# One decode step of windowed attention and a SwiGLU branch: Q, gate and up turned by VectorE's block transposes, and the last two rows of W_O in fifteen small loads

## The chip, the cores and the metric

The kernel runs on one core of a Trainium2 chip. The metric is the device time of one execution in microseconds (us); the kernel before takes 202.76 us, the median of three runs (201.81 to 202.96).

## The reference

Four sequences, one new token each, hidden size 512. The token is normalised; an attention branch over the last 4096 positions of a cache and a gated feed-forward branch both start from it, and the sum with x is the result.

```python
# x: [4,1,512]; caches: [4, 8 kv heads, 16384, 128]; 32 query heads; F = 1792; all bfloat16
xn = layernorm(x)
q = (xn @ wq) as 32 heads of 128                    # wq: [512, 4096]
k, v = last 4096 positions of the caches, each kv head for 4 query heads
p = softmax(q @ k.T * 128 ** -0.5)
a = (p @ v) as [4, 4096] @ wo                       # wo: [4096, 512]
f = (silu(xn @ w_gate) * (xn @ w_up)) @ w_down      # w_gate, w_up: [512, 1792]; w_down: [1792, 512]
out = x + a + f
```

## The kernel before

**Loads.** SyncE issues nearly all DMA from one queue, in a written order: W_Q (4 MB), K of steps 0 and 1, W_gate, W_up, V of step 0, then K and V in turn, W_down, V of the last step in two halves, and W_O in four loads (`load_wo`, L231) of its row groups 0 to 15, 16 to 25, 26 to 29 and 30 to 31 (`WO_CUTS`, L121). A row group c is `WO[:, c, :]`: 128 partitions of 512 values, so the last load is 128 partitions of 2 KB. K and V have two buffers each; a K load waits until the transposes of two steps before are done (`s_tr`), a V load until PV of two steps before is done (`s_pv`).

**Start.** ScalarE and VectorE normalise x, TensorE turns it, and `XnT` holds it with hidden along the partitions and 32 columns, of which 4 are the tokens. Q is computed in 32 matmuls (L370 to L375) with `XnT` stationary and 512 columns of W_Q moving; four of them write the four 32-partition groups of a PSUM tile, so that the tokens are in partitions 32j to 32j+3. ScalarE and VectorE copy the two tiles to `QB`, eight TensorE transposes turn them, and four VectorE copies sort them into `QZ` (L293 to L296).

**Loop.** 16 steps (`ND`), each with one kv head of two sequences, 64 tiles of 128 positions. TensorE transposes K tile by tile into four PSUM tiles, VectorE copies them to `KT` (`evac`, L299), TensorE forms the scores; a maximum, a shift and ScalarE's exponential follow, and PV (`pv`, L413) adds P x V and the denominators. `norm` (L316) divides. The order of every engine is written out by hand, with a semaphore for each dependence.

**End.** After the last scores TensorE computes gate and up into `ps_kt[0]` and `ps_kt[1]` (L452 to L460). Column f of W_gate is seen as (m, t) with f = 14 m + t. Each of the four partition groups gets four of the 14 values of t, `T0[j]` to `T0[j] + 3` (groups 2 and 3 overlap in two), so a matmul moves 128 runs of four neighbours, 14 apart, in 512 columns. ScalarE takes exp(-gate); VectorE adds 1, takes the reciprocal, multiplies by gate and by up (L337 to L345), all on 128 partitions x 512 columns of which 4 partitions in 32 are tokens. Meanwhile TensorE does the last step's PV; then four transposes turn `gu` (L467), four turn the attention output (L471), VectorE copies both (`OB`, `guT`), four matmuls with `rep` spread the heads (L477), VectorE copies `OP`. The 28 matmuls with W_down (L483) and the 64 with W_O (L490) add into `ps_acc`, on two groups of columns side by side. Before row groups 0, 16, 26 and 30 of W_O TensorE waits for the load that brings them (L491). VectorE copies the sum to `y`, and SyncE and ScalarE store a half each.

Of the kernel before, what the change touches and what calls it, by code (L numbers as in the profile page):

```python
# [3 lines left out]
BF16 = mybir.dt.bfloat16  # L4
FP32 = mybir.dt.float32
# [5 lines left out]
def bass_parallel_sum__sliding_block_cached__swiglu_ffn__decode_kernel(  # L11
# [67 lines left out]
    st_std = sb("st_std", [B, 1], FP32)  # L79
    st_rstd = sb("st_rstd", [B, 1], FP32)  # L80
    XnT = sb("xnT", [128, NC, 32], BF16)
    QB = sb("qB", [128, 2, 512], BF16)
    den = sb("den", [128, C], FP32)
    OT = sb("oT", [128, B, REP + HQ], BF16)
    OB = sb("oB", [32, B, Dh], BF16)
    OP = sb("oP", [128, NO, B], BF16)
    ex = WQ[:, 0:1024].bitcast(FP32)
    gu = sb("gu", [128, 4, 128], BF16)
    guT = sb("guT", [128, 4, 128], BF16)
    I4 = sb("i4", [B, B], FP32)  # L90
    I4w = sb("i4w", [B, 64], BF16)
    y = sb("y_sb", [128, 256], BF16)
# [9 lines left out]
    O_wide = ps_O[:, 0:WIDE]  # L102
    den_ps = ps_O[:, 128:256]
    xT_ps = ps_acc[:, 0:NC * B]
    q_ps = kt_ps[2]
    mt_ps = ps_acc[0:C, 0:128]
    gate_ps = ps_kt[0][:]
    up_ps = ps_kt[1][:]
    gu_ps = kt_ps[2][:, B:2 * B, :]
    tr_ps = kt_ps[2][0:32, 0:B, :]  # L110
    op_ps = ps_kt[3][:, 0:B * 32]

    def sem(name):
        return nc.alloc_semaphore(name=name)
# [4 lines left out]
    d_wd = sem("d_wd")  # L119
    d_out = sem("d_out")  # L120
    WO_CUTS = (0, 16, 26, 30, 32)  # L121
    d_wo = [sem("d_wo%d" % q) for q in range(len(WO_CUTS) - 1)]
    d_k = [sem("d_k%d" % s) for s in range(2)]
    d_v = [sem("d_v%d" % s) for s in range(2)]
    d_vz = sem("d_vz")
# [7 lines left out]
    s_xT = sem("s_xT")  # L133
    s_xnT = sem("s_xnT")
    s_q = sem("s_q")
    s_qb = sem("s_qb")
    s_qt = sem("s_qt")
    s_gu = sem("s_gu")
    s_gt = sem("s_gt")
    s_qz = sem("s_qz")  # L140
    s_tr = sem("s_tr")
# [33 lines left out]
    with nc.Block() as block:  # L175
# [40 lines left out]
        @block.sync  # L216
        def _(eng):
            def load_k(d):
                if d >= 2:
                    eng.wait_ge(s_tr, 2 * NG * (d - 1))  # L220
                eng.dma_start(KB[:, d % 2 * KVN:(d % 2 + 1) * KVN], kv_ap(A_k_cache, d)).then_inc(d_k[d % 2], 16)

            def load_v(d):
                eng.wait_ge(s_pv, d + 1)
                eng.dma_start(VB[:, d % 2 * KVN:(d % 2 + 1) * KVN], kv_ap(A_v_cache, d)).then_inc(d_v[d % 2], 16)

            def load_v_half(d, h, done):
                a = d % 2 * KVN + h * HKN
                eng.dma_start(VB[:, a:a + HKN], kv_ap(A_v_cache, d)[:, :, h * HKN:(h + 1) * HKN]).then_inc(done, 16)

            def load_wo(n):  # L231
                a, b = WO_CUTS[n], WO_CUTS[n + 1]
                eng.dma_start(WO[:, a:b, :], wo_ap[:, a:b, :]).then_inc(d_wo[n], 16)

            eng.dma_start(WQ[:], wq_ap).then_inc(d_wq, 16)
            load_k(0)
            load_k(1)
            eng.dma_start(WG[:], wg_ap).then_inc(d_wg, 16)
            eng.dma_start(WU[:], wu_ap).then_inc(d_wu, 16)
            load_v(0)  # L240
            for d in range(2, ND):
                load_k(d)
                load_v(d - 1)
            eng.dma_start(WD[:], wd_ap).then_inc(d_wd, 16)
            eng.wait_ge(s_pv, ND)
            load_v_half(ND - 1, 0, d_v[1])
            load_v_half(ND - 1, 1, d_vz)
            for n in range(len(d_wo)):
                load_wo(n)
            eng.wait_ge(s_y, 1)  # L250
            eng.dma_start(out_ap[0], y[0:B, :]).then_inc(d_out, 16)
            eng.wait_ge(d_out, 32)

        @block.scalar
        def _(eng):
            eng.dma_start(X[:], x_ap).then_inc(d_x, 16)
            eng.wait_ge(s_xc, 1)
            eng.activation(xc[:], X[:], ACT.Identity, bias=st_neg[:, 0:1], scale=float(D))
            eng.drain()
            eng.activation(xsq[:], xc[:], ACT.Square, accum_out=st_sum[:, 0:1]).then_inc(s_ss, 1)  # L260
            eng.wait_ge(s_var, 1)
            eng.activation(st_std[:], st_var[:], ACT.Sqrt).then_inc(s_std, 1)
            eng.wait_ge(s_rs, 1)
            eng.activation(xn[:], xc[:], ACT.Identity, scale=st_rstd[:, 0:1]).then_inc(s_xn, 1)  # L264
            eng.wait_ge(s_q, 1)
            eng.activation(QB[:, 0, :], ps_kt[0][:], ACT.Identity).then_inc(s_qb, 1)
            for d in range(-1, ND):
                eng.wait_ge(s_sh, d + 2)
                eng.activation(P[:, d % 2 * PS:d % 2 * PS + SN], ps_S[d % 2][:], ACT.Exp, scale=SCALE).then_inc(s_p, 1)  # L269
            eng.wait_ge(s_gate, 1)  # L270
            eng.activation(ex, gate_ps, ACT.Exp, scale=-1.0).then_inc(s_ex, 1)  # L271
            eng.wait_ge(s_y, 1)
            eng.dma_start(out_ap[1], y[64:64 + B, :]).then_inc(d_out, 16)

        @block.vector
        def _(eng):
# [6 lines left out]
            eng.wait_ge(s_xT, 1)  # L283
            eng.wait_ge(s_const, 1)
            eng.tensor_copy(XnT[:, :, 0:B], xT_ps.rearrange("p (c b) -> p c b", b=B)).then_inc(s_xnT, 1)
            eng.wait_ge(s_q, 1)
            eng.tensor_copy(QB[:, 1, :], ps_kt[1][:]).then_inc(s_qb, 1)  # L287
            eng.wait_ge(s_qt, 1)

            qv = q_ps.rearrange("p (n h) (j x) -> p j n x h", n=2, x=32)  # L290
            qz = QZ[:].rearrange("p (j n i) c -> p j n i c", n=2, i=2)
            for n in range(2):
                for i in range(2):  # L293
                    last = eng.tensor_copy(qz[:, :, n, i, 0:C].rearrange("p j (m h) -> p j m h", m=2),  # L294
                                           qv[:, :, n, 2 * i:2 * i + 2, :])
            last.then_inc(s_qz, 1)  # L296
            eng.engine_nop().then_inc(s_ev, NG)

# [27 lines left out]
            with eng.Fori(0, ND // 2) as r:  # L326
                for b in range(2):
# [5 lines left out]
            row_max(1, ND + 1)  # L333
            shift(ND + 1)
            norm(ND + 1, 0, ND // 2)
            eng.wait_ge(s_ex, 1)
            eng.tensor_scalar(ex, ex, 1.0, None, ALU.add)  # L337
            eng.drain()
            eng.reciprocal(ex, ex)  # L339
            eng.drain()  # L340
            eng.tensor_tensor(ex, gate_ps, ex, ALU.mult)  # L341
            eng.wait_ge(s_up, 1)
            eng.drain()
            eng.tensor_tensor(gu[:].rearrange("p u m -> p m u"), up_ps.rearrange("p (m u) -> p m u", u=4),  # L344
                              ex.rearrange("p (m u) -> p m u", u=4), ALU.mult).then_inc(s_gu, 1)  # L345
            norm(ND + 2, 1, ND // 2)

            eng.wait_ge(s_t4, 1)
            eng.tensor_copy(OB[:], tr_ps).then_inc(s_ob, 1)
            eng.wait_ge(s_gt, 1)  # L350
            eng.tensor_copy(guT[:], gu_ps).then_inc(s_guT, 1)
            eng.wait_ge(s_pm, 1)
            eng.tensor_copy(OP[:].rearrange("p c b -> p b c"), op_ps.rearrange("p (b c) -> p b c", b=B)).then_inc(s_op, 1)
            eng.wait_ge(s_acc, 1)
# [3 lines left out]
        def _(eng):  # L358
# [8 lines left out]
            last.then_inc(s_xT, 1)  # L367
            eng.wait_ge(s_xnT, 1)
            eng.wait_ge(d_wq, 16)
            for c in range(NC):  # L370
                for n in range(2):
                    for j in range(4):
                        a = (c * HQ + 8 * j + 4 * n) * Dh
                        last = mm(ps_kt[n][32 * j:32 * j + 32, :], XnT[:, c, :], WQ[:, a:a + 512], start=(c == 0))
            last.then_inc(s_q, 1)  # L375
            eng.wait_ge(s_qb, 2)
            for k in range(8):
                last = eng.transpose(q_ps[:, k, :], QB[:, k // 4, 128 * (k % 4):128 * (k % 4 + 1)], ident[:])  # L378
            last.then_inc(s_qt, 1)

            def mask(bank):
                return mm(ps_S[bank][:].rearrange("p (t c) -> p t c", c=C), mkr[:],
# [65 lines left out]
            pv(0, 1, ND + 1)  # L448
            shift(1, ND + 1)


            T0 = (0, 4, 8, NF - 4)  # L452
            for w, o, done, d in ((WG, ps_kt[0], s_gate, d_wg), (WU, ps_kt[1], s_up, d_wu)):
                eng.wait_ge(d, 16)
                for c in range(NC):
                    wv = w[:, c, :].rearrange("p (m t) -> p m t", t=NF)
                    for j in range(4):
                        last = mm(o[32 * j:32 * j + 32, :].rearrange("p (m u) -> p m u", u=4), XnT[:, c, :],
                                  wv[:, :, T0[j]:T0[j] + 4], start=(c == 0))
                last.then_inc(done, 1)  # L460
            for n in range(2):
                mm(ps_acc[64 * n:64 * n + 64, 0:256], I4w[:], X[:, 256 * n:256 * n + 256], start=True)
            pv(1, 0, (8 * ND + 16, ND + 1))
            eng.wait_ge(d_vz, 16)
            pv(1, 1, None)
            eng.wait_ge(s_gu, 1)
            for u in range(4):  # L467
                last = eng.transpose(gu_ps[:, u, :], gu[:, u, :], ident[:])
            last.then_inc(s_gt, 1)
            eng.wait_ge(s_nrm, ND + 2)  # L470
            for i in range(B):  # L471
                last = eng.transpose(
# [5 lines left out]
                last = mm(op_ps.rearrange("p (b c) -> p b c", b=B), rep[:, e, :], OB[:, :, 32 * e:32 * e + 32],  # L478
                          start=(e == 0))
            last.then_inc(s_pm, 1)  # L480
            eng.wait_ge(s_guT, 1)
            eng.wait_ge(d_wd, 16)
            for t in range(NF):  # L483
                j = min(t // 4, 3)
                u = t - T0[j]
                for n in range(2):
                    mm(ps_acc[64 * n:64 * n + B, 0:256], guT[:, u, 32 * j:32 * j + B],
                       WD[:, t, 256 * n:256 * n + 256])
            eng.wait_ge(s_op, 1)
            for c in range(NO):  # L490
                if c in WO_CUTS:  # L491
                    eng.wait_ge(d_wo[WO_CUTS.index(c)], 16)
                for n in range(2):
                    last = mm(ps_acc[64 * n:64 * n + B, 0:256], OP[:, c, :], WO[:, c, 256 * n:256 * n + 256])
# [29 lines left out]
```

## Time and profile before

| | before |
|---|---|
| runs, us | 202.96, 202.76, 201.81 (median 202.76) |
| profiled execution, us | 203.49, of which the span of instructions 201.8 |
| granted TensorE clock, mean | 0.958 |
| HBM read | 81.01 MB, 402 GB/s over the span |
| busy share | PE 83%, PE weight loads 71%, VectorE 59%, ScalarE 9%, GpSimd 5% |
| chain that ended last | DMA 51%, PE 40%, VectorE 6%, issue 2% |

The span is the time from the first to the last instruction that the profiler records in one execution; the profiled execution's own time has some 1.7 us more around it. Busy shares are averages over stages with different limits. The chain is followed back from the last instruction, at each step to what released it. A line such as L360 is a helper's (`mm`), so groups are told apart by their tiles.

### The profile page before, as it was taken

The page shows a single profiled execution, that of the slowest core. Times are in us where ns is not written, and L with a number is a line of the kernel's source. Part 1 is how long each engine was busy: PE and PEld are TensorE (multiplying, and loading weights), DVE is VectorE, ACT ScalarE, POOL GpSimd, SP SyncE. Part 2 cuts the span into 40 slices and gives each one's busy share as a digit, 9 for nine tenths or more (in the row PEclk, how much of TensorE's full clock was granted, in tenths as well). Part 3 has the DMA queues.
Part 4 walks back from the last instruction along what each step waited for, and adds up shares of the span by engine and source line. Part 5 has one row for each costly group of instructions (what it writes and reads, how often), then busy time and mean ns, then how long its engine had stood idle before and what let it go on. Part 6 is the DMA issues. An engine that isn't in the chain of part 4 may idle for free.

```text
span 201.8 us, 7765 instructions
## 1 busy us (share of the span) xinstructions
PE 167.1 (83%) x3470; PEld 143.2 (71%) x3470; DVE 119.3 (59%) x250; ACT 17.6 (9%) x27; POOL 10.3 (5%) x23
## 2 busy tenths in 40 slices
PE   0137998859999989889898989898989898986395
PEld 0113896758988978788788878887878787854263
DVE  1003757644777575757666767676767676738700
ACT  6303010101010101010100101010101010110000
POOL 8920000000000000000000000000000000000000
PEclk9999699988999999999999999999999999999559
DMA  7999999999999999999999999999999999999800
GB/s 248 448 393 429 436 424 426 437 422 429 406 426 439 435 422 439 432 422 435 432 432 426 439 435 422 439 432 422 435 432 432 426 439 435 413 435 421 373 12 1
DMA packets 5934, 81.10 MB, mean 402 GB/s; under 512 B 668, under 2 KB 680, under 8 KB 936
## 3 DMA queue, kind: packets, MB, share of 16 engines
q1 hardware_dynamic: 5912, 81.01, 94.4%
q8 instruction: 5, 0.08, 0.2%
q10 hardware_dynamic: 16, 0.01, 0.0%
q14 instruction: 1, 0.01, 0.0%
HBM read 81.01 MB, written 0.00 MB: 402 GB/s over the span
## 4 chain that ended last, share of the span: by engine, by line
DMA 51%; PE 40%; DVE 6%; issue 2%; ACT 0%; DVEq 0%
DMA kbuf<-in_A_k_cache_dram 44%; PE ps_kt L390 17%; PE ps_s L360 9%; DMA wq_sb<-in_A_wq_dram 6%; PE ps_o L360 6%; PE ps_acc L360 5%; PE ps_kt L360 3%; DVE wq_sb L339 2%; DVE kT L302 1%; DVE gu L344 1%; DVE rm L307 0%; DVE qB L287 0%; DVE wq_sb L341 0%; PE ps_kt L378 0%; ACT wq_sb L271 0%
## 5 line engine op out<-in xcount | busy, mean ns | idle before, releaser
L302 DVE COPY kT<-ps_kt 128x1024 bf16<-128x1024 bf16 x128 | 79.8, 683 | 27.3 <-PE ps_kt L390 27.2
L390 PE MATMUL ps_kt<-ident,kbuf 128*128 128x128 bf16 x1024 | 64.4, 222 | 10.6 <-DMA kbuf<-in_A_k_cache_dram 10.5
L390 PEld LDWEIGHTS ps_kt<-ident,kbuf 128*128 128x128 bf16 x1024 | 58.8, 99 | 15.6 <-issue 15.6
L360 PE MATMUL ps_o<-p,vbuf 128*128 128x64 bf16 x1120 | 39.4, 195 | 0.0
L360 PEld LDWEIGHTS ps_o<-p,vbuf 128*128 128x128 bf16 x1120 | 36.2, 99 | 1.2
L360 PEld LDWEIGHTS ps_s<-qz,kT 128*128 128x128 bf16 x1024 | 31.4, 98 | 7.6 <-issue 4.6
L360 PE MATMUL ps_s<-qz,kT 128*128 x1024 | 34.8, 192 | 2.0 <-issue 0.8
L269 ACT ACTIVATE p<-ps_s 128x512 bf16<-128x512 f32 x17 | 10.2, 597 | 152.0 <-PE ps_s L360 152.0
L307 DVE TENSOR_REDUCE rm<-ps_s 128x8 bf16<-128x512 f32 x17 | 11.8, 691 | 19.3 <-PE ps_s L360 19.3
L360 PE MATMUL ps_kt<-wq_sb,xnT 128*32 128x512 bf16 x32 | 3.4, 609 | 5.4 <-DMA wq_sb<-in_A_wq_dram 5.4
L360 PE MATMUL ps_o<-p,ones 128*128 128x128 bf16 (+1 forms) x69 | 6.9, 220 | 0.8 <-DVE qz L294 0.7
L360 PE MATMUL ps_s<-mkc,mkr 2*128 2x512 bf16 x17 | 6.7, 393 | 0.0
L365 PE MATMUL ps_acc<-i,xn 4*128 4x4 f32 x4 | 0.6, 255 | 7.2 <-ACT xn L264 7.2
L360 PE MATMUL ps_s<-dg,ones 8*128 8x512 bf16 x17 | 6.5, 385 | 0.0
L360 PEld LDWEIGHTS ps_kt<-wq_sb,xnT 128*32 128x32 bf16 x32 | 1.3, 140 | 6.9 <-issue 6.9
L318 DVE TENSOR_REDUCE den<-ps_o 128x8 f32<-128x128 f32 x18 | 5.1, 281 | 1.6 <-PE ps_o L360 1.6
L287 DVE CAST qB<-ps_kt 128x512 bf16<-128x512 f32 x1 | 0.7, 691 | 8.7 <-PE ps_kt L360 8.7
L365 PEld LDWEIGHTS ps_acc<-i,xn 4*128 4x128 f32 x4 | 0.6, 210 | 7.2 <-issue 7.2
L360 PEld LDWEIGHTS ps_o<-p,ones 128*128 128x128 bf16 x69 | 4.5, 98 | 1.3 <-issue 0.8
L211 POOL MEMSET vbuf<- 128x6144 f32 x1 | 5.2, 5222 | 0.0
L360 PE MATMUL ps_acc<-wo_sb,oP 128*4 128x256 bf16 x64 | 5.1, 334 | 0.0
L355 DVE CAST y_sb<-ps_acc 128x256 bf16<-128x256 f32 x1 | 0.4, 426 | 7.5 <-PE ps_acc L360 7.5
(69 smaller groups left out, 62.7 us busy)
## 6 DMA issues: line engine op xcount, KB each, us to landing
kbuf<-in_A_k_cache_dram SPq DMA_DIRECT2D x16, 2048.0 KB, 12.6
vbuf<-in_A_v_cache_dram SPq DMA_DIRECT2D x15, 2048.0 KB, 11.2
wq_sb<-in_A_wq_dram SPq DMA_DIRECT2D x1, 4096.0 KB, 12.3
vbuf<-in_A_v_cache_dram SPq DMA_DIRECT2D x2, 1024.0 KB, 9.2
wo_sb<-in_A_wo_dram SPq DMA_DIRECT2D x1, 2048.0 KB, 14.5
wg_sb<-in_B_w_gate_dram SPq DMA_DIRECT2D x1, 1792.0 KB, 25.8
wu_sb<-in_B_w_up_dram SPq DMA_DIRECT2D x1, 1792.0 KB, 29.4
wd_sb<-in_B_w_down_dram SPq DMA_DIRECT2D x1, 1792.0 KB, 15.0
```

The lines of the kernel that those rows point to most:

```text
L211: eng.memset(VB[:, HKN:].bitcast(FP32), 0.0)
L269: eng.activation(P[:, d % 2 * PS:d % 2 * PS + SN], ps_S[d % 2][:], ACT.Exp, scale=SCALE).then_inc(s_p, 1)
L287: eng.tensor_copy(QB[:, 1, :], ps_kt[1][:]).then_inc(s_qb, 1)
L302: eng.tensor_copy(KT[:, u * HKN + 1024 * g:u * HKN + 1024 * (g + 1)], kt_ps[g].rearrange("p a b -> p (a b)")).then_inc(s_ev, 1)
L307: eng.tensor_reduce(RM[:], ps_S[bank][:].rearrange("p (t c) -> p c t", c=C), AX.X, ALU.max).then_inc(s_rm, 1)
L318: eng.tensor_reduce(den[:], den_ps.rearrange("p (t c) -> p c t", c=C), AX.X, ALU.add)
L339: eng.reciprocal(ex, ex)
L344: eng.tensor_tensor(gu[:].rearrange("p u m -> p m u"), up_ps.rearrange("p (m u) -> p m u", u=4), ex.rearrange("p (m u) -> p m u", u=4), AL ...
L355: eng.tensor_copy(y[:], ps_acc[:, 0:256]).then_inc(s_y, 1)
L360: return eng.matmul(o, l, r, start=start, stop=stop, skip_group_check=True)
L365: last = eng.transpose(xT_ps[:, c * B:(c + 1) * B], xn[:].rearrange("b (p c) -> b c p", c=NC)[:, c, :], I4[:])
L390: last = eng.transpose(kt_ps[g][:, k, :], KB[:, a:a + 128], ident[:])
```

## The change

Q's matmuls are ordered by PSUM tile first, and each 32-partition group now holds 16 heads x 32 of their 128 dimensions. VectorE's 32 x 32 block transpose takes each PSUM tile straight to `qT` in fp32 (in the space of `KT`), so that dimensions lie along partitions and 4 of every 32 columns are tokens; two copies sort it into `QZ`. `QB`, its two copies and the eight TensorE transposes go.

Gate and up hold, for each of the four partition groups, m from 32j to 32j+31 and all 14 t: 448 columns, with a step of 14 elements between neighbours in the weights. VectorE block-transposes gate to `gT` and up to `uT` (in the space of `WQ`); ScalarE's exponential and VectorE's four operations then work on 14 x 4 = 56 columns, and the product is `guT` itself. The four TensorE transposes of `gu` and the copy go. The matmuls with W_down move ahead of the transposes of the attention output, and the exponential waits for `gT` in place of the gate matmuls.

The fourth load of W_O is replaced by 15 loads of 2, 3, ... 15 and 9 partitions (128 together), each with its own semaphore; TensorE waits for all 15 ahead of row group 30.

```diff
@@ tiles
-    QB = sb("qB", [128, 2, 512], BF16)
-    ex = WQ[:, 0:1024].bitcast(FP32)
-    gu = sb("gu", [128, 4, 128], BF16)
-    guT = sb("guT", [128, 4, 128], BF16)
+    ex = sb("ex", [128, NF, B], FP32)
+    guT = sb("guT", [128, NF, B], BF16)
+    qT = KT[:, 0:2048].bitcast(FP32)
+    gT = WQ[:, 0:NF * 64].bitcast(FP32)
+    uT = WQ[:, NF * 64:NF * 128].bitcast(FP32)
...
-    gate_ps = ps_kt[0][:]
-    up_ps = ps_kt[1][:]
-    gu_ps = kt_ps[2][:, B:2 * B, :]
+    gate_ps = ps_kt[0][:, 0:NF * 32]
+    up_ps = ps_kt[1][:, 0:NF * 32]
@@ semaphores
-    d_wo = [sem("d_wo%d" % q) for q in range(len(WO_CUTS) - 1)]
+    d_wo = [sem("d_wo%d" % q) for q in range(len(WO_CUTS) - 2)]
+    LAST = tuple(range(2, 16)) + (9,)
+    d_last = [sem("d_last%d" % q) for q in range(len(LAST))]
@@ sync
             for n in range(len(d_wo)):
                 load_wo(n)
+            p = 0
+            for n, k in enumerate(LAST):
+                eng.dma_start(WO[p:p + k, WO_CUTS[-2]:, :], wo_ap[p:p + k, WO_CUTS[-2]:, :]).then_inc(d_last[n], 16)
+                p += k
@@ scalar
-            eng.wait_ge(s_q, 1)
-            eng.activation(QB[:, 0, :], ps_kt[0][:], ACT.Identity).then_inc(s_qb, 1)
...
-            eng.wait_ge(s_gate, 1)
-            eng.activation(ex, gate_ps, ACT.Exp, scale=-1.0).then_inc(s_ex, 1)
+            eng.wait_ge(s_gt, 1)
+            eng.activation(ex[:], gT.rearrange("p (t b) -> p t b", b=32)[:, :, 0:B], ACT.Exp, scale=-1.0).then_inc(s_ex, 1)
@@ vector
-            eng.wait_ge(s_q, 1)
-            eng.tensor_copy(QB[:, 1, :], ps_kt[1][:]).then_inc(s_qb, 1)
-            eng.wait_ge(s_qt, 1)
-            qv = q_ps.rearrange("p (n h) (j x) -> p j n x h", n=2, x=32)
-            qz = QZ[:].rearrange("p (j n i) c -> p j n i c", n=2, i=2)
             for n in range(2):
-                for i in range(2):
-                    last = eng.tensor_copy(qz[:, :, n, i, 0:C].rearrange("p j (m h) -> p j m h", m=2),
-                                           qv[:, :, n, 2 * i:2 * i + 2, :])
+                eng.wait_ge(s_q, n + 1)
+                eng.transpose(qT[:, 512 * n:512 * n + 512], ps_kt[n][:])
+            eng.drain()
+            for i in range(2):
+                last = eng.tensor_copy(
+                    QZ[:].rearrange("p (k i) c -> p k i c", i=2)[:, :, i, 0:C].rearrange("p k (m h) -> p k m h", m=2),
+                    qT.rearrange("p (k h x) -> p k x h", h=REP, x=32)[:, :, 2 * i:2 * i + 2, :])
...
             norm(ND + 1, 0, ND // 2)
+            eng.wait_ge(s_gate, 1)
+            eng.transpose(gT, gate_ps).then_inc(s_gt, 1)
+            eng.wait_ge(s_up, 1)
+            eng.transpose(uT, up_ps)
             eng.wait_ge(s_ex, 1)
-            eng.tensor_scalar(ex, ex, 1.0, None, ALU.add)
+            eng.tensor_scalar(ex[:], ex[:], 1.0, None, ALU.add)
...
-            eng.tensor_tensor(ex, gate_ps, ex, ALU.mult)
-            eng.wait_ge(s_up, 1)
+            eng.tensor_tensor(ex[:], gT.rearrange("p (t b) -> p t b", b=32)[:, :, 0:B], ex[:], ALU.mult)
             eng.drain()
-            eng.tensor_tensor(gu[:].rearrange("p u m -> p m u"), up_ps.rearrange("p (m u) -> p m u", u=4),
-                              ex.rearrange("p (m u) -> p m u", u=4), ALU.mult).then_inc(s_gu, 1)
+            eng.tensor_tensor(guT[:], uT.rearrange("p (t b) -> p t b", b=32)[:, :, 0:B], ex[:],
+                              ALU.mult).then_inc(s_guT, 1)
             norm(ND + 2, 1, ND // 2)
...
-            eng.wait_ge(s_gt, 1)
-            eng.tensor_copy(guT[:], gu_ps).then_inc(s_guT, 1)
@@ tensor
-            for c in range(NC):
-                for n in range(2):
+            for n in range(2):
+                for c in range(NC):
+                    wv = WQ[:, c * HQ * Dh:(c + 1) * HQ * Dh].rearrange("p (n h d) -> p n h d", n=2, d=Dh)
                     for j in range(4):
-                        a = (c * HQ + 8 * j + 4 * n) * Dh
-                        last = mm(ps_kt[n][32 * j:32 * j + 32, :], XnT[:, c, :], WQ[:, a:a + 512], start=(c == 0))
-            last.then_inc(s_q, 1)
-            eng.wait_ge(s_qb, 2)
-            for k in range(8):
-                last = eng.transpose(q_ps[:, k, :], QB[:, k // 4, 128 * (k % 4):128 * (k % 4 + 1)], ident[:])
-            last.then_inc(s_qt, 1)
+                        last = mm(ps_kt[n][32 * j:32 * j + 32, :].rearrange("p (h d) -> p h d", d=32), XnT[:, c, :],
+                                  wv[:, n, :, 32 * j:32 * j + 32], start=(c == 0))
+                last.then_inc(s_q, 1)
...
-                    wv = w[:, c, :].rearrange("p (m t) -> p m t", t=NF)
+                    wv = w[:, c, :].rearrange("p (m t) -> p t m", t=NF)
                     for j in range(4):
-                        last = mm(o[32 * j:32 * j + 32, :].rearrange("p (m u) -> p m u", u=4), XnT[:, c, :],
-                                  wv[:, :, T0[j]:T0[j] + 4], start=(c == 0))
+                        last = mm(o[32 * j:32 * j + 32, :].rearrange("p (t m) -> p t m", t=NF), XnT[:, c, :],
+                                  wv[:, :, 32 * j:32 * j + 32], start=(c == 0))
...
             pv(1, 1, None)
-            eng.wait_ge(s_gu, 1)
-            for u in range(4):
-                last = eng.transpose(gu_ps[:, u, :], gu[:, u, :], ident[:])
-            last.then_inc(s_gt, 1)
+            eng.wait_ge(s_guT, 1)
+            eng.wait_ge(d_wd, 16)
+            for t in range(NF):
+                for n in range(2):
+                    mm(ps_acc[64 * n:64 * n + B, 0:256], guT[:, t, :], WD[:, t, 256 * n:256 * n + 256])
             eng.wait_ge(s_nrm, ND + 2)
...
-            eng.wait_ge(s_guT, 1)
-            eng.wait_ge(d_wd, 16)
-            for t in range(NF):
-                j = min(t // 4, 3)
-                u = t - T0[j]
-                for n in range(2):
-                    mm(ps_acc[64 * n:64 * n + B, 0:256], guT[:, u, 32 * j:32 * j + B],
-                       WD[:, t, 256 * n:256 * n + 256])
             eng.wait_ge(s_op, 1)
             for c in range(NO):
-                if c in WO_CUTS:
+                if c == WO_CUTS[-2]:
+                    for done in d_last:
+                        eng.wait_ge(done, 16)
+                elif c in WO_CUTS:
                     eng.wait_ge(d_wo[WO_CUTS.index(c)], 16)
```

More of the change, by code (lines that the diff above doesn't have):

```diff
@@ L104, in bass_parallel_sum__sliding_block_cached__swiglu_ffn__decode_kernel @@
     xT_ps = ps_acc[:, 0:NC * B]
-    q_ps = kt_ps[2]
     mt_ps = ps_acc[0:C, 0:128]
-    gate_ps = ps_kt[0][:]
-    up_ps = ps_kt[1][:]
-    gu_ps = kt_ps[2][:, B:2 * B, :]
+    gate_ps = ps_kt[0][:, 0:NF * 32]
+    up_ps = ps_kt[1][:, 0:NF * 32]
     tr_ps = kt_ps[2][0:32, 0:B, :]
@@ L135, in bass_parallel_sum__sliding_block_cached__swiglu_ffn__decode_kernel @@
     s_q = sem("s_q")
-    s_qb = sem("s_qb")
-    s_qt = sem("s_qt")
-    s_gu = sem("s_gu")
     s_gt = sem("s_gt")
@@ L335, in _ @@
             norm(ND + 1, 0, ND // 2)
+            eng.wait_ge(s_gate, 1)
+            eng.transpose(gT, gate_ps).then_inc(s_gt, 1)
+            eng.wait_ge(s_up, 1)
+            eng.transpose(uT, up_ps)
             eng.wait_ge(s_ex, 1)
-            eng.tensor_scalar(ex, ex, 1.0, None, ALU.add)
+            eng.tensor_scalar(ex[:], ex[:], 1.0, None, ALU.add)
             eng.drain()
-            eng.reciprocal(ex, ex)
+            eng.reciprocal(ex[:], ex[:])
             eng.drain()
-            eng.tensor_tensor(ex, gate_ps, ex, ALU.mult)
-            eng.wait_ge(s_up, 1)
+            eng.tensor_tensor(ex[:], gT.rearrange("p (t b) -> p t b", b=32)[:, :, 0:B], ex[:], ALU.mult)
             eng.drain()
-            eng.tensor_tensor(gu[:].rearrange("p u m -> p m u"), up_ps.rearrange("p (m u) -> p m u", u=4),
-                              ex.rearrange("p (m u) -> p m u", u=4), ALU.mult).then_inc(s_gu, 1)
+            eng.tensor_tensor(guT[:], uT.rearrange("p (t b) -> p t b", b=32)[:, :, 0:B], ex[:],
+                              ALU.mult).then_inc(s_guT, 1)
             norm(ND + 2, 1, ND // 2)
@@ L449, in _ @@
             shift(1, ND + 1)
-            T0 = (0, 4, 8, NF - 4)
-            for w, o, done, d in ((WG, ps_kt[0], s_gate, d_wg), (WU, ps_kt[1], s_up, d_wu)):
+            for w, o, done, d in ((WG, gate_ps, s_gate, d_wg), (WU, up_ps, s_up, d_wu)):
                 eng.wait_ge(d, 16)
                 for c in range(NC):
-                    wv = w[:, c, :].rearrange("p (m t) -> p m t", t=NF)
+                    wv = w[:, c, :].rearrange("p (m t) -> p t m", t=NF)
                     for j in range(4):
-                        last = mm(o[32 * j:32 * j + 32, :].rearrange("p (m u) -> p m u", u=4), XnT[:, c, :],
-                                  wv[:, :, T0[j]:T0[j] + 4], start=(c == 0))
+                        last = mm(o[32 * j:32 * j + 32, :].rearrange("p (t m) -> p t m", t=NF), XnT[:, c, :],
+                                  wv[:, :, 32 * j:32 * j + 32], start=(c == 0))
                 last.then_inc(done, 1)
```

## The prediction

> **What bounds the kernel now.** I read the page's slices first, then busy time by stage, then the timeline of the last 22 us and the landings of the last loads. In the slices the clock that TensorE was granted is full nearly throughout and halves near the end:
>
> ```profile
> PEclk9999699988999999999999999999999999999559
> ```
>
> The stages (columns: stretch, its length, busy us and instructions of PE, weight loads, VectorE, ScalarE and GpSimd, granted clock, DMA share, GB/s):
>
> ```profile
> 20.00:30.00 10.00, 9.92 (x197) 8.93 (x195) 6.44 (x15) 0.60 (x1) 0.00 (x0) 0.84 1.00 426
> 28.00:190.00 162.00, 144.23 (x3185) 127.34 (x3181) 109.17 (x225) 10.15 (x17) 0.00 (x0) 0.98 1.01 429
> 187.00:197.00 10.00, 7.23 (x66) 4.46 (x68) 3.77 (x7) 0.00 (x0) 0.00 (x0) 0.50 0.44 179
> 190.00:191.00 1.00, 0.49 (x5) 0.23 (x4) 0.55 (x2) 0.00 (x0) 0.00 (x0) 0.50 0.90 356
> 191.00:192.00 1.00, 1.00 (x10) 0.61 (x12) 0.64 (x2) 0.00 (x0) 0.00 (x0) 0.50 0.37 145
> 192.00:193.00 1.00, 1.00 (x14) 0.63 (x10) 0.00 (x1) 0.00 (x0) 0.00 (x0) 0.50 0.11 27
> ```
>
> From 20 to 190 us the DMA engines are full (share 1.00, 1.01): this stretch is set by bytes. The share then falls to 0.37 and 0.11: the engines do not finish together. After that comes a tail that DMA no longer sets. Its timeline (start, length, engine and line, operation):
>
> ```profile
> 179.87 0.29 DVE L318 TENSOR_REDUCE den<-ps_o 128x8 f32<-128x128 f32 x1 [0.47 <-PE ps_o L360]
> 180.08 1.33 PE L360 MATMUL ps_kt<-wg_sb,xnT 128*32 128x512 bf16 x16
> 180.51 0.17 DVE L322 TENSOR_TENSOR oT<-ps_o,den 128x8 bf16<-128x8 f32 x1
> 182.50 0.29 PE L360 MATMUL ps_acc<-x_sb,i4w 4*64 4x256 bf16 x2
> 182.58 3.35 DVE L339 RECIPROCAL wq_sb<-wq_sb 128x512 f32<-128x512 f32 x1
> 182.97 2.03 PE L360 MATMUL ps_o<-p,vbuf 128*128 128x64 bf16 x64
> 186.78 2.43 DVE L344 TENSOR_TENSOR gu<-ps_kt,wq_sb 128x512 bf16<-128x512 f32 x1
> 189.27 0.61 PE L468 MATMUL ps_kt<-ident,gu 128*128 128x128 bf16 x4 [4.27 <-DVE gu L344]
> 189.80 0.61 PE L472 MATMUL ps_kt<-ident,oT 128*32 128x128 bf16 x4
> 190.45 0.41 DVE L349 COPY oB<-ps_kt 32x512 bf16<-32x512 bf16 x1 [0.70 <-PE ps_kt L472]
> 190.92 0.60 PE L360 MATMUL ps_kt<-oB,rep 32*128 32x128 bf16 x4 [0.51 <-DVE oB L349]
> 191.45 3.15 PE L360 MATMUL ps_acc<-wd_sb,guT 128*4 128x256 bf16 x28
> 191.56 0.44 DVE L353 CAST oP<-ps_kt 128x128 bf16<-128x128 f32 x1 [0.36 <-PE ps_kt L360]
> 194.39 5.08 PE L360 MATMUL ps_acc<-wo_sb,oP 128*4 128x256 bf16 x64
> 199.52 0.43 DVE L355 CAST y_sb<-ps_acc 128x256 bf16<-128x256 f32 x1 [7.52 <-PE ps_acc L360]
> ```
>
> PV ends at 185.0 (182.97 + 2.03), and TensorE then stands 4.27 us until VectorE has walked 512-column tensors: the reciprocal alone 3.35, the product 2.43. The clock halves from 187 on, and the 92 matmuls of W_down and W_O run mostly at half speed: 28 in 194.39 - 191.45 = 2.94 us, 0.105 each. Of W_O's 64, 28 fit at that rate before 197.3; the other 36 take 1.9 us more up to the last matmul's start at about 199.2: 0.053 each at full clock.
>
> When W_O lands (issues with KB and us to landing; then the issue times; then the queues' packets):
>
> ```profile
> wo_sb<-in_A_wo_dram SPq DMA_DIRECT2D x1, 2048.0 KB, 14.5
> wo_sb<-in_A_wo_dram SPq DMA_DIRECT2D x1, 1280.0 KB, 16.9
> wo_sb<-in_A_wo_dram SPq DMA_DIRECT2D x1, 512.0 KB, 17.7
> wo_sb<-in_A_wo_dram SPq DMA_DIRECT2D x1, 256.0 KB, 17.8
> L233 SPq DMA_DIRECT2D wo_sb<-in_A_wo_dram x4: 432/436/593, 173.2 to 174.8; - x4
> q1 hardware_dynamic: 5912, 81.01, 94.4%
> q10 hardware_dynamic: 16, 0.01, 0.0%
> ```
>
> Issued at 173.2, 173.8, 174.3 and 174.8, they land whole at 187.7, 190.7, 192.0 and 192.6. W_O's rows are used in that order (0 to 15, to 25, to 29, to 31).
>
> **The gate path, the main term.** After the change VectorE transposes gate and up (448 columns each) and then works on 56 columns. No row shows the transpose. A dense pass over 512 fp32 columns of PSUM is the nearest:
>
> ```profile
> L287 DVE CAST qB<-ps_kt 128x512 bf16<-128x512 f32 x1 | 0.7, 691 | 8.7 <-PE ps_kt L360 8.7
> L360 PE MATMUL ps_kt<-wg_sb,xnT 128*32 128x512 bf16 x16 | 1.3, 453 | 0.0
> L360 PE MATMUL ps_s<-dg,ones 8*128 8x512 bf16 x17 | 6.5, 385 | 0.0
> ```
>
> I take 0.65 for one transpose and four times that as the upper bound. The reciprocal shrinks with its columns, 3.35 x 56/512 = 0.37; the three other small operations stay near the 0.17 of an oT product. Up's transpose, these and their gaps end about 1.7 us after up's last matmul. ScalarE's exponential of gate lies beside up's matmuls. PV ends 185.0 - 182.4 = 2.6 us after up's last matmul, so TensorE finds guT ready; only a transpose above 1.5 us would show. The wait of 4.27 goes, with the four transposes (0.61) and the guT copy.
>
> **What gate and up cost on TensorE.** The moving rows now step 14 elements (28 bytes) for every element; before, four neighbours were read at each step. Before, 512 columns of four-element runs cost 453 ns against 385 for 512 unspaced ones: 68 ns more for 128 runs, 0.53 per run. Four column groups work at once, and gate and up take 2.3 us for 8 steps (180.08 to 182.4, just ahead of the matmul at 182.50), so 0.285 a step. After, the dense part: W_O's matmuls run in pairs side by side, 256 columns in 2 x 0.053 = 0.107, so 448 columns take 0.187. With 448 x 0.53 ns = 0.238 for the steps that is 0.425 a step of four, **3.4 us** for eight, 1.1 more than now. Lower bound: nothing beyond the columns saved, 0.25 a step, 2.0 in all. Upper bound: a run of one as dear as a run of four (0.285/128 = 2.2 ns), 1.0 a step, 8.0 in all. I take 3.4, which leaves the dense rate where the 385 row has it.
>
> [...]
>
> **The rest of the tail**, at full clock: up ends 183.5, PV 186.1. W_down's 28 matmuls, moved ahead of the output transposes, take 28 x 0.053 = 1.5, to 187.6. norm (179.87 to 180.68, 0.8) lies beside them; before, W_down covered only the OP copy (0.44), which is now bare. Then four transposes 0.4, OB 0.43, four replications 0.4, OP 0.46 (the PE groups at about two thirds of their half-clock 0.6): W_O can start at 189.3. Its 64 matmuls take 3.4: row 16 is reached at 191.0 (landed 190.7), row 26 at 192.1 (192.0), row 30 at 192.5, where the last load, 192.6, is due. So **DMA sets the end by a hair**: last matmuls out at 193.0, 6.5 us before the present 199.5.
>
> **The last two rows in 15 loads.** Queue 1 holds 41 loads of 128 rows and a store of 4; 41 x (128 + 16) + 8 = 5912; queue 10 has two transfers of 4 rows, 2 x (4 + 4) = 16. So a transfer of 4 rows has 4 completions, one of 128 has 16: I read that a load of k < 16 rows runs on k engines. Data packets stay 128; completions become 128 instead of 16. From third to fourth landing an engine did 8 packets of 2 KB and a completion in 0.6 us: under 0.08 a packet all in. If every load starts at the same engine, one engine has 15 packets and another none, in place of 8 each. Is the early engine the loaded one, all could level at 191.5 (191 plus the remaining 0.37 + 0.11 us of share); is the late one loaded, 192.6 + 7 x 0.08 = 193.2; unknown which, I keep 192.6. Rows 26 to 29 wait for the third load until 192.0 and take 0.4 anyway, so the best case gains 0.2 us at most, the worst costs 0.6. SyncE issues 14 more DMAs; at 0.43 to 0.59 each the 15 are out before 184, seven us ahead of their bytes, and only the stores queue behind them. TensorE's 15 waits stand behind matmuls already queued; I put them at 0 to 0.3.
>
> **The start.** Q's path loses a PSUM copy, eight transposes and two of four copies, and gets two transposes, the first beside matmuls. At most the 1.9 us between Q's matmuls and QZ is at stake:
>
> ```profile
> 16.75 0.69 DVE L287 CAST qB<-ps_kt 128x512 bf16<-128x512 f32 x1 [8.69 <-PE ps_kt L360]
> 18.16 0.48 DVE L294 COPY qz<-ps_kt 128x32 bf16<-128x32 bf16 x4 [0.72 <-PE ps_kt L378]
> 24.01 0.55 SPq L225 DMA_DIRECT2D vbuf<-in_A_v_cache_dram  x1
> 27.58 0.54 SPq L221 DMA_DIRECT2D kbuf<-in_A_k_cache_dram  x1
> ```
>
> I count 0: the first loads that wait for compute are issued at 24.01 and 27.58 into a queue that is full, and the bytes ahead of them do not move. If a transpose took four times my price, the start would come some 4 us later and the queue would still be fed. Q's runs of 32 elements are read as now.
>
> **Sum.** 203.49 of the profiled execution (span 201.8 and 1.7 around it) - 6.5 = **197.0**. The median of the runs, 202.76, is lower than the profiled one; I ascribe that to where the half-clock stretch happened to end. The new end hangs on DMA, so I take nothing more off: 197.0 against 202.76.
>
> **Rivals.** *Lone elements are dear* (0.27): at 5 to 8 us for gate and up every step behind moves along, and the end is 1.6 to 4.6 us later, 198.6 to 201.6. [...] Against it: nothing measured here.
>
> *The clock falls again* (0.14):
>
> ```profile
> 16.40:19.81 3.41, 1.94 (x27) 1.14 (x20) 1.57 (x6) 1.88 (x2) 0.00 (x0) 1.00 1.02 437
> 156.34:159.76 3.42, 2.56 (x73) 2.36 (x70) 1.56 (x4) 0.00 (x0) 0.00 (x0) 1.00 1.01 431
> 183.65:187.06 3.41, 1.34 (x47) 1.22 (x42) 3.26 (x3) 0.00 (x0) 0.00 (x0) 1.00 0.95 408
> ```
>
> A stretch of 3.41 us with 1.34 or 1.94 busy was followed by half clock, one with 2.56 was not. My new tail has two waits of 0.45, so about 2.5 busy of 3.41, more loss if W_O's rows come late. If it falls at row 16, up to 32 matmuls cost 0.053 more: 1.7 us, about 198.5. [...]
>
> *Slower* (0.05): each completion holds its engine before the next packet. Then the engine with 15 packets, done with the third load at 191 to 192, decides the end. From 0.5 us a packet on, the last load lands at 199 and the gain is gone; at 0.6 it lands at 200.0 at the earliest, 7.4 after 192.6, and the kernel takes 204.4. For it: no row shows completions one behind another. Against it: the 0.6 us for eight packets and one completion.
>
> *The change does not reach the end* (0.04): something I do not see keeps the tail where it is, 202 to 203.
>
> **Numbers.** The forecast itself has 0.50 (196.3 to 197.7, from the last landing's two bounds and the waits). With the clock rival and the cheaper half of the dear reads (to 6.4 us, 200.0) the range 196.3 to 200.0 holds 8 in 10. A measurement tells about 0.5%, 1.0 us. The forecast, the clock and nearly all of the dear reads are faster by more: 0.90; same 0.05; slower 0.05.
>
> **What would show it.** Gate and up: mean and spacing of their matmuls. The transposes: their rows. guT ready before PV's end: no TensorE wait ahead of W_down. The clock: 1.00 from 187 on. W_O: TensorE's last idle time put down to wo_sb, last landing 191.5 to 193.2. Wrong would be a gate stage beyond 6.4 us, a transpose beyond 1.5, or a last landing beyond 194.

## The result, and the profile after

The changed kernel takes 200.31 us (median of 5 runs, 199.94 to 200.37), the kernel before 202.76 (201.81 to 203.04). The ratio is 0.988, 95% interval 0.985 to 0.991: faster, clear of noise, but by 2.45 us and not by the 5.8 forecast, and 0.3 us above the upper end of the range. The profiled execution took 199.94 us with a span of 198.2, before 203.49 and 201.8.

The slices of the page, and busy time by stage (columns as before):

```profile
PEclk9999999657999999999999999999999999999999
```

```profile
28.00:190.00 162.00, 148.21 (x3130) 127.70 (x3129) 103.69 (x225) 9.81 (x17) 0.00 (x0) 0.97 1.01 429
185.00:196.00 11.00, 9.93 (x179) 6.67 (x170) 3.18 (x10) 0.00 (x0) 0.00 (x0) 1.00 0.58 237
```

The long middle is as it was, share 1.01 and 429 GB/s; the dip in the slices, at 35 to 50 us, lies in it, where bytes set the time. In the tail TensorE is now busy 9.93 us of 11, and its clock stays full (1.00) where it was halved before (0.50). The timeline of that tail:

```profile
179.96 3.42 PE L361 MATMUL ps_kt<-wg_sb,xnT 128*32 128x448 bf16 x16
180.75 0.13 PEld L361 LDWEIGHTS ps_kt<-wg_sb,xnT 128*32 128x32 bf16 x4 [0.67 <-issue]
181.56 0.13 PEld L361 LDWEIGHTS ps_kt<-wg_sb,xnT 128*32 128x32 bf16 x4 [0.68 <-issue]
183.17 3.44 PE L361 MATMUL ps_kt<-wu_sb,xnT 128*32 128x448 bf16 x16
183.41 0.65 DVE L337 STREAM_TRANSPOSE wq_sb<-ps_kt 128x448 f32<-128x448 f32 x1 [2.85 <-PE ps_kt L361]
186.65 0.65 DVE L339 STREAM_TRANSPOSE wq_sb<-ps_kt 128x448 f32<-128x448 f32 x1 [2.58 <-PE ps_kt L361]
187.00 2.03 PE L361 MATMUL ps_o<-p,vbuf 128*128 128x64 bf16 x64
187.45 0.50 DVE L343 RECIPROCAL ex<-ex 128x56 f32<-128x56 f32 x1
188.32 0.22 DVE L347 TENSOR_TENSOR guT<-wq_sb,ex 128x56 bf16<-128x56 f32 x1
188.96 1.69 PE L361 MATMUL ps_acc<-wd_sb,guT 128*4 128x256 bf16 x28
191.81 0.44 DVE L354 CAST oP<-ps_kt 128x128 bf16<-128x128 f32 x1 [0.49 <-PE ps_kt L361]
192.31 3.66 PE L361 MATMUL ps_acc<-wo_sb,oP 128*4 128x256 bf16 x64 [0.53 <-DVE oP L354]
196.01 0.42 DVE L356 CAST y_sb<-ps_acc 128x256 bf16<-128x256 f32 x1 [3.75 <-PE ps_acc L361]
```

VectorE's 6.9 us of 512-column work (0.43, 3.35, 0.69 and 2.43) are gone, guT is ready at 188.5 and TensorE does not wait for it. But gate and up, 2.3 us before, now take from 179.96 to 186.5: 6.5 us. The weight loads show the rhythm, four every 0.80 us, and it was forecast at 0.425. Everything behind is as long as forecast and 3 us later, so W_O's loads have all landed before its rows are used: the last of them at 194.4, while row group 30 starts at about 195.5.

### The profile page after: what moved, and what is told of

Same layout as the page of the kernel before. It is cut to its first block, busy times and chain, and to the rows that moved or that the text cites. A ratio compares the mean times of both kernels' runs of the same rounds, so it can differ in the third digit from the quotient of the medians.

```text
span 198.2 us, 7762 instructions
## 1 busy us (share of the span) xinstructions
PE 167.0 (84%) x3458; PEld 142.0 (72%) x3458; DVE 115.0 (58%) x250; ACT 16.6 (8%) x26; POOL 10.3 (5%) x23
## 3 DMA queue, kind: packets, MB, share of 16 engines
q1 hardware_dynamic: 6024, 81.01, 96.1%
## 4 chain that ended last, share of the span: by engine, by line
DMA 52%; PE 41%; DVE 3%; issue 2%; DVEq 0%
DMA kbuf<-in_A_k_cache_dram 46%; PE ps_kt L389 17%; PE ps_s L361 9%; PE ps_o L361 7%; DMA wq_sb<-in_A_wq_dram 6%; PE ps_kt L361 5%; PE ps_acc L361 4%; DVE kT L301 1%; DVE kT L289 0%; DVE rm L306 0%; DVE oP L354 0%; DVE y_sb L356 0%; DVE oB L352 0%; DVE qz L292 0%; PE ps_kt L470 0%
## 5 line engine op out<-in xcount | busy, mean ns | idle before, releaser
L361 PEld LDWEIGHTS ps_s<-qz,kT 128*128 128x128 bf16 x1024 | 32.1, 99 | 6.7 <-issue 3.7
L361 PE MATMUL ps_s<-qz,kT 128*128 x1024 | 35.3, 193 | 1.2
L289 DVE STREAM_TRANSPOSE kT<-ps_kt 128x512 f32<-128x512 f32 x2 | 1.4, 718 | 7.9 <-PE ps_kt L361 7.9
L311 DVE TENSOR_REDUCE m<-ps_acc 8x1 f32<-8x128 f32 x17 | 4.6, 269 | 0.3 <-PE ps_acc L361 0.3
L321 DVE TENSOR_TENSOR oT<-ps_o,den 128x8 f32 (+1 forms) x18 | 3.0, 167 | 2.9 <-issue 2.7
```

Source lines behind the costliest of these rows:

```text
L289: eng.transpose(qT[:, 512 * n:512 * n + 512], ps_kt[n][:])
L311: eng.tensor_reduce(m8[:], mt_ps, AX.X, ALU.max)
L321: eng.tensor_tensor(OT[:, 2 * b:2 * b + 2, ds(r * REP, REP)], O_ps.rearrange("p (j h) -> p j h", j=2), den[:].rearrange("p (j h) -> p j h" ...
L361: return eng.matmul(o, l, r, start=start, stop=stop, skip_group_check=True)
```

## The experiments

My first theory: the whole miss lies in TensorE reading every 14th element of W_gate and W_up; the small last loads land late but are hidden behind it. Rivals: the output or the number of matmuls is dear, the loads or their 15 waits hold the end, or the start is worth something.

**e1_dense15: neighbours read, the picking done by the transposes.**

```diff
-                    wv = w[:, c, :].rearrange("p (m t) -> p t m", t=NF)
-                        last = mm(o[32 * j:32 * j + 32, :].rearrange("p (t m) -> p t m", t=NF), XnT[:, c, :], wv[:, :, 32 * j:32 * j + 32], ...)
+                        last = mm(o[32 * j:32 * j + 32, :], XnT[:, c, :], w[:, c, 448 * j:448 * j + 448], ...)
-            eng.transpose(gT, gate_ps).then_inc(s_gt, 1)
+            eng.transpose(gT.rearrange("p (t b) -> p t b", b=32), gate_ps.rearrange("p (m t) -> p t m", t=NF)).then_inc(s_gt, 1)
             (up and uT likewise)
```

> Gate and up read 448 neighbouring columns; the block transposes pick every 14th column of PSUM instead. Theory (lone strided reads made gate and up 6.5 us long in place of 3.4, and this alone put the end of the work 3 us behind the forecast): gate and up take 1.6 us, PV ends near 184.1, W_O can start near 187.4 and waits for its loads. With the 15 small loads landing as late as in the changed kernel (194.4, completions 0.2 us apart) the end is near 198.6; rival on the loads (landing as before, 192.6): 197.0. Rival on the reads (the matmuls' output or their number is dear, not the reading): gate and up stay at 6.5 us and the time at 200.3. If the transpose pays for picked columns as the old gu product did (2.4 us), TensorE waits some 0.5 us for guT and nothing else changes.

**e2_dense1: the same, and the last two rows of W_O in one load again.**

```diff
-            for n, k in enumerate(LAST):
-                eng.dma_start(WO[p:p + k, WO_CUTS[-2]:, :], ...).then_inc(d_last[n], 16)
+            (the fourth load_wo, 128 partitions, and one wait)
```

> As e1_dense15, with the last two rows of W_O in one load of 128 partitions again. If the small loads' completions are what lands late: last landing 192.6, end near 197.0, 1.5 us faster than e1_dense15. If they are harmless: same as e1_dense15. If TensorE's clock halves while it waits for W_O: near 198.5.

**e8_dense8: as e1, the last rows in 8 loads of 16 partitions.**

```diff
-    LAST = tuple(range(2, 16)) + (9,)
+    LAST = (16,) * 8
```

> As e1_dense15, with the last two rows in 8 loads of 16 partitions: every engine gets 8 packets and 8 completions, evenly. If completions cost (0.2 us for a packet with its own completion against 0.08 without): last landing 193.4 to 193.6, end near 198.0. If the unevenness of 2 to 15 was the cost: last landing 192.6, end near 197.0.

| kernel | median us (runs) | ratio to before, 95% interval |
|---|---|---|
| e1_dense15 | 199.08 (198.81 to 200.1) | 0.983 (0.981 to 0.986) |
| e8_dense8 | 198.53 (198.36 to 199.12) | 0.980 (0.978 to 0.983) |
| e2_dense1 | 197.43 (197.04 to 198.06) | 0.975 (0.973 to 0.977) |

The timeline of e1_dense15, then of e8_dense8 and e2_dense1 from W_O's rows on (of W_O's matmuls the `x4` are rows 30 and 31, the `x8` rows 26 to 29):

```profile
180.13 0.94 PE L361 MATMUL ps_kt<-wg_sb,xnT 128*32 128x448 bf16 x16
180.90 0.93 PE L361 MATMUL ps_kt<-wu_sb,xnT 128*32 128x448 bf16 x16
181.13 0.65 DVE L337 STREAM_TRANSPOSE wq_sb<-ps_kt 128x448 f32<-128x448 f32 x1 [0.39 <-PE ps_kt L361]
187.75 1.91 PE L361 MATMUL ps_acc<-wo_sb,oP 128*4 128x256 bf16 x32 [0.75 <-DMA wo_sb<-in_A_wo_dram]
192.40 0.60 PE L361 MATMUL ps_acc<-wo_sb,oP 128*4 128x256 bf16 x8 [0.22 <-DMA wo_sb<-in_A_wo_dram]
194.65 0.38 PE L361 MATMUL ps_acc<-wo_sb,oP 128*4 128x256 bf16 x4 [1.64 <-DMA wo_sb<-in_A_wo_dram]
```

```profile
192.48 0.31 PEld L361 LDWEIGHTS ps_acc<-wo_sb,oP 128*4 128x4 bf16 x8 [0.35 <-DMA wo_sb<-in_A_wo_dram]
194.18 0.38 PE L361 MATMUL ps_acc<-wo_sb,oP 128*4 128x256 bf16 x4 [1.10 <-DMA wo_sb<-in_A_wo_dram]
```

```profile
187.75 1.91 PE L354 MATMUL ps_acc<-wo_sb,oP 128*4 128x256 bf16 x32 [0.87 <-DMA wo_sb<-in_A_wo_dram]
190.70 2.21 PE L354 MATMUL ps_acc<-wo_sb,oP 128*4 128x256 bf16 x32 [1.04 <-DMA wo_sb<-in_A_wo_dram]
191.91 0.31 PEld L354 LDWEIGHTS ps_acc<-wo_sb,oP 128*4 128x4 bf16 x8 [0.25 <-DMA wo_sb<-in_A_wo_dram]
192.52 0.09 PEld L354 LDWEIGHTS ps_acc<-wo_sb,oP 128*4 128x4 bf16 x4 [0.30 <-DMA wo_sb<-in_A_wo_dram]
```

Dense reading takes gate and up to 1.6 us, and a transpose that picks every 14th column costs the same 0.65. Now W_O waits for DMA, and the last loads decide: row 30 starts 0.61 us after row 26 with one load, 1.70 with 8 and 2.25 with 15 (a weight load and its matmul start within 0.03 us of each other). Eight even loads are nearly as late as 15 uneven ones, so the unevenness is not the main cost.

The trace's records of the landings say more. In e8_dense8 the eight loads complete at 192.65, 192.84, 193.04 and so on to 194.05, **0.20 us apart**, though the last 2 KB packet starts at 192.52; in e1_dense15 the last ten complete from 192.69 to 194.51, 0.20 apart as well, and in the changed kernel from 192.56 to 194.37, with the last 2 KB packet at 192.41. A small load's completions, one for each of its partitions, do not come together: those of the changed kernel's load of 15 partitions come from 191.47 to 194.17. So I take the 0.20 for the spacing of completions on one DMA engine; that is inferred, since no run varied the loads and their completions separately. It is more than 8 loads were expected to cost: the last was expected at 193.4 to 193.6. The load ahead of them suffers too: it lands at 191.87 with one load behind it, at 192.44 with 8 and at 192.36 with 15. Why, no run shows.

One load is 1.65 us better than 15 by the medians, and e2_dense1 is the best version of all, 0.4 us from the forecast. That closeness is partly luck: its gate and up take 1.6 us where the forecast had 3.4, and TensorE spends the time gained waiting for W_O.

**e3_one: the changed kernel with one last load** (the edit of e2 alone).

> The changed kernel with the last two rows of W_O in one load, all else as changed. TensorE reaches row 30 at 195.5, after either landing (192.6 or 194.4), so both theories on the loads give the changed kernel's time, 200.3 within 0.4. If the 15 waits themselves cost TensorE time, it would be up to 0.6 faster.

Measured 200.22 (200.09 to 200.31; ratio 0.988, 0.986 to 0.990): no difference. In the changed kernel the small loads cost nothing, and the 15 waits neither.

**e5_steps: single elements 2 apart (gate) and 4 apart (up).**

```diff
+            for w, o, done, d, k in ((WG, gate_ps, s_gate, d_wg, 2), (WU, up_ps, s_up, d_wu, 4)):
...
+                        last = mm(o[32 * j:32 * j + 32, :], XnT[:, c, :], (448 elements, k apart), start=(c == 0))
```

A line is here 16 neighbouring bytes, and a hit an element read in it; the size of 16 and the price were assumptions, which this run and the next put to the test.

> Gate reads 448 single elements 2 apart (4 bytes), up 4 apart (8 bytes); which columns they are is wrong, so the result is left out. Price by 16-byte lines (one line costs four dense elements' time, whatever is used of it): gate 4 hits a line, near 0.2 us per four matmuls, up 2 hits a line, near 0.4, against 0.805 for lone elements 14 apart. Price by address step: 0.8 for both.

**e6_pairs_alone: pairs 14 apart (gate); lone elements, written one column group after the other (up).**

```diff
+                wv = WG[:, c, :].rearrange("p (m k t) -> p k m t", k=NF // 2, t=2)
...
-                for c in range(NC):
-                    for j in range(4):
+            for j in range(4):
+                for c in range(NC):
```

> Gate reads pairs of neighbours 14 apart (224 runs of 2; the order of columns differs, so the result is left out); up reads lone elements as the changed kernel but one column group after the other, so that no two of its matmuls run side by side. Gate: by lines or runs 0.40 per four matmuls; by my recorded price (dense part and 0.53 ns a run) 0.31. Up: if the four groups share one supply of lines, a matmul alone is about four times faster, 0.2, and up takes as long as in the changed kernel, 3.2 us; if every stream is slow by itself, 0.8 a matmul, 12.9 us.

**e4_psum: neighbours read, PSUM written 32 columns apart.**

```diff
-   mm(o[32 * j:32 * j + 32, :].rearrange("p (t m) -> p t m", t=NF), XnT[:, c, :], wv[:, :, 32 * j:32 * j + 32], ...)
+   mm(o[32 * j:32 * j + 32, :].rearrange("p (t m) -> p m t", t=NF), XnT[:, c, :], (448 neighbours, as m t), ...)
```

> Gate and up read neighbouring columns and write PSUM every 32 columns (128 bytes apart) in place of that; transposes as in the changed kernel. If only the reading is dear: 0.2 per four matmuls, 1.6 us for gate and up, as e1_dense15. If spread writes are as dear as spread reads: 0.8 and the changed kernel's time.

The groups of gate and up (mean ns of one matmul), of the changed kernel, e1_dense15, e5_steps, e6_pairs_alone and e4_psum in this order:

```profile
L361 PE MATMUL ps_kt<-wg_sb,xnT 128*32 128x448 bf16 x16 | 3.4, 984 | 0.0
```

```profile
L361 PE MATMUL ps_kt<-wg_sb,xnT 128*32 128x448 bf16 x16 | 0.9, 355 | 0.0
```

```profile
L361 PE MATMUL ps_kt<-wu_sb,xnT 128*32 128x448 bf16 x16 | 1.8, 577 | 0.0
L361 PE MATMUL ps_kt<-wg_sb,xnT 128*32 128x448 bf16 x16 | 1.0, 362 | 0.0
```

```profile
L361 PE MATMUL ps_kt<-wu_sb,xnT 128*32 128x448 bf16 x16 | 3.4, 987 | 0.0
L361 PE MATMUL ps_kt<-wg_sb,xnT 128*32 128x448 bf16 x16 | 1.8, 580 | 0.0
```

```profile
L361 PE MATMUL ps_kt<-wg_sb,xnT 128*32 128x448 bf16 x16 | 1.7, 573 | 0.0
```

A dense matmul streams its 448 columns in 0.187 us, so some 0.17 of the 0.355 is fixed, and the rest is streaming. Singles 4 apart (448 address steps, two to 16 bytes) cost as much as pairs 14 apart (224 steps), 577 and 580; singles 2 apart, four to 16 bytes, are as good as dense. A price by address step is out. So is one that is added to the dense time, since singles 2 apart touch 112 stretches of 16 bytes and take only 7 ns more than dense ones. Counted in stretches of 16 bytes, lone elements touch 448 and stream 0.81 us, pairs and step 4 touch 224 and stream 0.41, and the old runs of four touched 160 (one run in four lies across two) in 0.285: **1.8 ns for each stretch in all of them**. Counted in 8 bytes, singles 4 apart would touch as many stretches as lone elements, 448, and took 577 ns against 984; counted in 32, they would touch 112 to the pairs' 196, and took the same (577 and 580). Spread writes into PSUM cost too: 573 ns against 355, a third of what spread reads add (984 against 355). That lies between the two values expected. One run each of e4_psum, e5_steps and e6_pairs_alone took 199.0, 198.91 and 199.08 us, as e1_dense15: all four then wait for the small loads.

**e10_one_group: spread reading for one column group (gate) and two (up).** Up's 16 matmuls in e6 took 3.4 us in all, not 12.9. (A column group here is the matmuls that write one of the four 32-partition groups of a PSUM tile.) I read that as one supply shared by the groups, at 0.2 us a matmul, and tested it:

```diff
-                    for j in range(4):
+                    for j in range(g):       # g = 1 for gate, 2 for up
```

> The changed kernel's spread reading, but gate is computed for one of the four column groups only (4 matmuls) and up for two (8); the rest of the gate and up columns is left out. If the groups share one supply of SBUF lines, a matmul by itself takes about 0.2 us however few groups there are: gate 0.8 us for its 4, up 0.2 apiece, 1.6 for its 8. If every stream of lone elements is slow by itself, four steps take as long as with all groups: 3.2 us for gate and 3.2 for up.

The timeline, and the two windows of 3.41 us on either side of 187.06, where the granted clock changed:

```profile
180.11 1.77 PE L361 MATMUL ps_kt<-wg_sb,xnT 128*32 128x448 bf16 x2
180.90 0.96 PE L361 MATMUL ps_kt<-wu_sb,xnT 128*32 128x448 bf16 x1
181.70 0.99 PE L361 MATMUL ps_kt<-wg_sb,xnT 128*32 128x448 bf16 x1
182.51 0.99 PE L361 MATMUL ps_kt<-wg_sb,xnT 128*32 128x448 bf16 x1
182.51 4.19 PE L361 MATMUL ps_kt<-wu_sb,xnT 128*32 128x448 bf16 x6
186.64 0.29 PE L361 MATMUL ps_acc<-x_sb,i4w 4*64 4x256 bf16 x2
```

```profile
183.64:187.06 3.42, 3.42 (x11) 0.54 (x9) 0.85 (x2) 0.25 (x1) 0.00 (x0) 1.00 0.97 411
187.06:190.47 3.41, 3.41 (x67) 3.41 (x65) 1.36 (x5) 0.00 (x0) 0.00 (x0) 0.50 0.97 399
```

The shared supply falls: a quarter of the matmuls of gate still takes 0.80 apiece, and both stages take 6.5 us (180.11 to 186.64) as with all groups. Each stream is slow by itself and four run side by side at no loss. How e6 ran four at once although they were written one group after the other: an up matmul here starts at 180.90, ahead of the last two gate matmuls, which stand before it in the program. So a matmul can overtake others. That it is one of another column group, and that this is what happened in e6, I infer, since the trace does not name column groups. The one run took 201.69 us, longer than the changed kernel with all its matmuls: the clock halved at 187.06, and PV took 3.56 us in place of 2.03.

**e7_oldq: the changed kernel with the old path of Q.**

```diff
-                eng.transpose(qT[:, 512 * n:512 * n + 512], ps_kt[n][:])
+            (QB, its two copies, eight transposes, four copies, as before)
```

> The changed kernel with the old path of Q (two copies, eight transposes, four copies). By the theory that the loads' bytes set the time up to 168 us: first K transposes 0.9 us later, end unchanged, 200.3 within 0.4. Rival (the shorter start is worth its 0.9 us): 201.2.

The starts of K's first transposes, e7_oldq and then the changed kernel:

```profile
20.18 3.59 PE L399 MATMUL ps_kt<-ident,kbuf 128*128 128x128 bf16 x32
29.02 0.54 SPq L223 DMA_DIRECT2D kbuf<-in_A_k_cache_dram  x1
```

```profile
18.34 1.96 PE L389 MATMUL ps_kt<-ident,kbuf 128*128 128x128 bf16 x32
25.09 0.54 SPq L220 DMA_DIRECT2D kbuf<-in_A_k_cache_dram  x1
```

Measured 200.1 (200.01 to 200.35; ratio 0.987, 0.984 to 0.989), the changed kernel's time, with K's first transposes 1.8 us later, twice what was expected, and the third K load issued 3.9 us later. The new Q path moves the start and not the end.

**e9_wd_late: W_down's matmuls behind the spreading of the heads again.**

```diff
             last.then_inc(s_pm, 1)
+            (waits for guT and W_down, 28 matmuls, as before)
```

> The changed kernel with W_down's matmuls behind the spreading of the heads again, as before the change. Then norm (0.8) stands bare behind PV and W_down covers the OP copy (0.46) instead. By that sum the end moves by 0.9 - 1.6 + 1.2 = within 0.4 of the changed kernel, 200.3. If the earlier place of W_down was itself a gain, it is slower by about 1 us.

Measured 200.53 (200.36 to 200.62; ratio 0.990, 0.987 to 0.992), 0.2 above the changed kernel: no difference within the intervals. The move alone is worth little, as the sum had it.

## Why the prediction was wrong

- **What bounds the kernel:** right. Bytes to 190 us (share 1.01 in both), then a tail of TensorE and VectorE.
- **The gate path:** right. A transpose took 0.65 as taken, the reciprocal 0.50 for 0.37, guT came 0.5 us ahead of PV's end, and the wait of 4.27 and the half clock went.
- **What gate and up cost on TensorE: this step failed.** It took the 68 ns that 128 runs cost beyond dense reading as 0.53 ns a run and added that to the dense time: 0.425 a step, 3.4 us. The runs show a price that replaces the dense time where it is longer, 1.8 ns for each 16-byte stretch and stream (one column group's reading): 448 of them, 0.81 a step, 6.5 us. The old runs of four lay only a third above the dense time (0.285 us a step against 0.21 for 512 dense columns), which made the price look small. The bounds, 2.0 and 8.0, did hold 6.5; the sum took a size nearer the lower one. Two elements read in 16 bytes stream at half the dense rate (577 ns against 355, of which some 0.17 us is fixed), four at the dense one (362). The change from 8 to 2 neighbouring bytes was in the diff, and the old step divided by its 160 stretches would have given the price, had the stretch been taken for the unit.
- **The rest of the tail:** right. From PV's end to W_O 3.2 us forecast, 192.31 - 189.03 = 3.3 measured; W_O's matmuls 3.4 and 3.7. **DMA sets the end by a hair** failed in the changed kernel, where TensorE sets it. Once the reading is dense and the last load is one, DMA does (e2_dense1, 197.43 against 197.0), and not by a hair: TensorE's waits for W_O add up to 1.9 us.
- **The last two rows:** the size was wrong and did not show. "Under 0.08 a packet all in" came from eight packets with one completion; with 112 completions more in the queue (6024 packets against 5912) the landings are 0.20 apart. The worst case was put at 193.2, and beyond 194 was to be a sign of being wrong: the last landing was 194.4 in the changed kernel and 194.5 in e1_dense15. In the changed kernel TensorE comes to row 30 later still, so e3_one finds nothing.
- **The start:** right, 0 (e7_oldq).
- **The rivals:** lone elements are dear (0.27) is what happened; at 6.5 us its own rule gives 200.1, measured 200.31. The range was cut at 6.4 us; its lower end, 196.3, does not follow from the sum, whose best case gains 0.2. The clock did not fall in the changed kernel's tail (1.00 from 185 to 196). The halving in e10_one_group, after a window with 3.42 of 3.42 us busy, shows that the busy time of TensorE's row does not decide it. What decides it, no run here shows. Small loads do land one behind another, as the slower rival had it, but 0.20 us apart and not the 0.5 from which the gain was lost.
- The 0.7 us between the profiled execution and the median of before was ascribed to the place of the half-clock stretch. No run tested it.

## What to carry to other kernels

Price a strided moving operand (bf16 here) by the 16-byte stretches that it touches, not by its elements, and take the larger of that and the dense time (here 1.8 ns a stretch, 0.42 ns a dense element). Where a layout needs a stride, look for who else can take it: here VectorE's block transpose picked every 14th column at no extra cost (0.65 us both ways), and TensorE read neighbours. Split a last load only where its completions have time: eight loads cost 1.1 us more than one (198.53 against 197.43), and it shows as soon as the compute ahead is quick enough to wait.

## What was not expected of the hardware

- A spread read takes 1.8 ns for each 16 bytes touched, at 2 or at 4 bytes used, and four column groups do this side by side without slowing each other (0.80 us for one matmul alone and for four).
- A matmul, by inference one of another column group, started before two that precede it in the program (180.90 against 181.70 and 182.51).
- Small loads in a row complete 0.20 us apart although their packets are through: the last packet starts at 192.52 and the last of eight loads completes at 194.05 (e8_dense8), at 192.41 and 194.37 in the changed kernel.
- Spread PSUM writes, 128 bytes apart, took 573 ns for a matmul of 448 columns against 355.
- The clock was halved (1.00 to 0.50) after a window in which TensorE's row was busy throughout (3.42 of 3.42 us), with one or two of four column groups at work.
